# An attention and mixture-of-experts kernel: the first routing's steps re-timed between two merged loops

## The chip, the cores and the metric

The program runs on one core of one Trainium2 chip: TensorE (PE), VectorE (DVE), ScalarE (ACT), GpSimd (POOL), and SyncE (SP) which here only issues DMAs. The metric is the device time of one execution in microseconds, the median of the runs shown.

## The reference, cut to what matters

Attention runs in chunks of 64 positions over 8 batches and 8 heads; its output is the input of a router that sends each of 4608 tokens to one of 8 experts, each of them two matrix products with a ReLU between.

```python
scores = scale * np.matmul(q_c, k_c.transpose(0, 1, 2, 4, 3))
attn = np.exp(scores - max); attn = attn / (sum + 1e-09)
x = np.matmul(attn, v_c) ...                      # 4608 x 512
logits = x @ w_gate + modality_bias[modality_id]  # 8 experts
e_idx, gate_w = argmax, its softmax weight
for e in range(E):
    h = np.maximum(x[mask] @ w1[e], 0.0)
    out[mask] = gate_w[mask, None] * (h @ w2[e])
```

## The kernel before, in words

The tokens are 36 tiles of 128; a **round** r does the attention of tiles 2r and 2r+1, so there are 18 rounds. A round has `scores` (64 small products, called one round ahead), `differences` (row maxima and the subtraction on VectorE), `exps` (ScalarE, and then one addition `sr` on GpSimd that halves the row to be summed), `sums` (the row sums and their reciprocals `ris`, VectorE), `transposes`, `values`, `evict` (ScalarE), `rows` (one for each of the two tiles: products that transpose back and give the router's partial logits, and a VectorE multiplication `xr` by `ris`), `parts` (ScalarE copies `lp` of the partial logits) and `put` (the tokens to the DRAM table `xd`). The first eight rounds (`NPURE`) run alone, and are called the **lone rounds** here. The other ten are emitted piecewise by the generator `merge`, between the products of the experts, three steps a round (transposes; values and the next scores; rows).

The experts work in **slots** of 384 tokens. Slot s has eight **blocks** f; the weight slice of block f of slot s is g = 8s + f. A block runs `first` (12 products, in two halves with a `tick` between, then ReLU and its low part `hh`, `hl`), `second` of the block before (9 products), and `wsplit(g + 3)`, which splits a weight slice fetched by `fetch` into a high and a low part. A `tick` runs what `later` has put off and takes one step of `merge`. All weights arrive by SP's queue in the order of the code, three pair buffers deep.

Routing is done for groups of tiles: 8, 8, 12 and 8 (`GROUPS`). Each has a generator, `route0` or `route(g)`, kept in the list `jobs`; `scatter(g, ...)`, kept in `pooljobs`, issues one indirect DMA a tile into the token table `tab` from GpSimd. `advance()` takes one step of each job and each pool job; in the lone rounds `hook(r, k)` calls it at four places k of a round, in a slot the blocks do. `route0` has these steps: the logits (L354), the maxima and the one-hot `oh0` (L357 to L362), the ranks (`rank_tiles`, L365 and L341 to L343, and then twenty VectorE operations to `vm`, L389), a pause, and `got` (eight products, L395) with two small operations that give slot 0's token list. Both products are put into the bank `pairs[1]`, which `rows` of the odd tiles uses too. `gather 0` (GpSimd, L717) then brings slot 0's rows, and `split 0` transposes them. After group 1 (`route(1)`) the generator `early_table(1)` makes, in four steps, the list of slots 1 to 3. `scatter(0)` writes to the table in one no-dependency group, `scatter(1)` in another (L507), so that a scatter of one group waits for those of the other that were emitted before it.

`PREP` names what is called at the end of a block: `choose` runs the jobs to their end, `blank` and `locate` are SP's DMAs on the table, `settle` ends the scatters, `gather 1` and `gather 2` bring the rows of slots 1 and 2 into the one buffer `xg`. `split 1 0` and `split 1 2` transpose slot 1's rows (6 products each on a bank of `pair()`, and a ScalarE and a VectorE pass); `AMID` puts them into the middle of a `first`. `pair()` alternates two PSUM banks, `spare()` takes one for the ranks of a later route. The order of the instructions on each engine is the order of the code.

Of the kernel before, what the change touches and what calls it, by code (L numbers as in the profile page):

```python
# [35 lines left out]
NPURE = 8  # L36
# [4 lines left out]
    7: {1: ["fetch 2"], 2: ["lo 0", "hi 1"]},  # L41
}
AHEAD = 3
AMID = {6: "split 1 0", 7: "split 1 2"}

PREP = {
    0: {2: ["choose", "blank 1"], 3: ["settle", "locate 1"],
        4: ["gather 1", "head"], 5: ["locate 2", "locate 3"], 7: ["gather 2"]},
# [48 lines left out]
def attention_moe(ctx: ExitStack, tc: tile.TileContext, qkv, mod, cst, bias, wcat, wfst, void, out):  # L97
# [236 lines left out]
    def logits(a, b):  # L334
        sums_of_heads(0, a, b - a, lg0[:, a:b])
# [9 lines left out]
    def route0():  # L345
# [6 lines left out]
            return wk.tile([P, n, E], dt, name=name, bufs=1)  # L352

        logits(6, n)  # L354
        yield
        mx, fm = t2("gmx0"), t2("fm0")
        V.reduce_max(mx, lg0, axis=AX.X)  # L357
# [417 lines left out]
    def fetch(g, n=2):  # L775
        s, f = divmod(g, NF)
        if s not in ereg:
            expert(s)
        raw = rawr[g // 2 % 3][:, f % 2:f % 2 + n]
        SP.dma_start(raw, (wfst if s < NSPLIT else wcat)[ds(ereg[s], 1), :, f:f + n, :].rearrange("e p f c -> p (e f) c"))  # L780
        for i in range(n):
            raws[g + i] = raw[:, i]
# [62 lines left out]
    def second(ys, h, w, f):  # L845
        whi, wlo = w
        hh, hl = h
        for t, y in enumerate(ys):
            tsl = slice(t * P, (t + 1) * P)
            for i, (a, b) in enumerate(((hh, whi), (hh, wlo), (hl, whi))):  # L850
                PE.matmul(y, a[:, tsl], b[:, DM:2 * DM],  # L851
                          start=(f == 0 and i == 0), stop=(f == NF - 1 and i == 2))
# [18 lines left out]
    def slot(s):  # L871

        nt = tiles(s)
        end = max(s + 1, NSURE) * NF
        ys = acc[0:nt]
        pend = None
        if s >= NSURE:
            expert(s)
            locate(s)
            for f in (0, 2, 4):  # L880
                fetch(s * NF + f)
            gather(s)
            stash(s)
            place(s)
            for f in range(AHEAD):
                wsplit(s * NF + f)
            for k in range(NK):
                turn(s, k)
                part(s, k)
        for f in range(NF):  # L890
            g = s * NF + f
            if s == 0 and f in (2, 3):
                if f == 3:
                    fetch(g + 5)
            elif f % 2 == 0 and g + 6 < end:
                fetch(g + 6)
            h = first(xring[s % 2], W[g], g, nt * P)
            tick()
            advance()
            if s == 0 and f < 4:  # L900
                for k in ((2,), (3,), (4,), (5, 6))[f]:
                    wsplit(k)
            elif g + AHEAD < end:
                wsplit(g + AHEAD)
            advance()
            if s == 0:
                advance()
            if pend is not None:
                second(ys, pend, W[g - 1], f - 1)
                tick()  # L910
            pend = h
            for c in PREP.get(s, REGULAR).get(f, ()) if s < NSURE else ():
                call(c, s if s > max(PREP) else 0)
            advance(pe=spare())
        second(ys, pend, W[s * NF + NF - 1], NF - 1)
        tick()
        finish(s, ys)

# [2 lines left out]
    jobs, pooljobs, due = [], [], []  # L921
# [5 lines left out]
    def advance(lists=None, pe=None):  # L927
        for js in lists or (jobs, pooljobs):
            for j in list(js):
                if j in held:  # L930
                    if pe is None:
                        continue
                    rpbank[0], pe = pe, None
                    held.discard(j)
                got = next(j, "end")
                if got == "end":
                    js.remove(j)
                elif got == "rp":
                    held.add(j)
# [9 lines left out]
    def tick():  # L949
        for d in due:  # L950
            d[0] -= 1
        for d in [d for d in due if d[0] <= 0]:
            due.remove(d)
            d[1](*d[2])
        if merging[0] and next(steps, "end") == "end":
            merging[0] = False
# [13 lines left out]
    def hook(r, k):  # L970
        clock[0] = r
        advance()
        for c in PLAN.get(r, {}).get(k, ()):
            call(c)
# [8 lines left out]
    for r in range(NPURE):  # L983
        scores(r + 1, sb)
        hook(r, 0)
        differences(r + 1, sb)
        hook(r, 1)
        transposes(r, ts)
        if r:
            rows(2 * r - 2, pairs[0])  # L990
        exps(r + 1)
        values(r, ts)
        hook(r, 2)
        if r:
            rows(2 * r - 1, pairs[1])
        evict(r)
        if r:
            parts(r - 1)
            put(r - 1)
        hook(r, 3)  # L1000
        sums(r)
        if r == 0:
            setup()
    clock[0] = NPURE
# [1 line left out]
    wlo(1)  # L1006
    split(0, 0, sb)
    split(0, 2, pairs[0])
    rows(2 * NPURE - 2, pairs[1])
    sums(NPURE)  # L1010

# [107 lines left out]
```

## Time and profile before

| | us |
|---|---|
| median of 3 runs | 566.47 |
| lowest, highest | 565.35, 567.4 |
| the profiled execution | 567.62 |
| its span, first to last instruction | 565.8 |
| PE busy | 526.5 (93%) |
| VectorE busy | 357.6 (63%) |
| ScalarE busy | 241.8 (43%) |
| GpSimd busy | 166.6 (29%) |
| mean granted clock of TensorE | 0.986 |

The lone rounds take the span's first 73.5 us, slot 0 the time to about 160 us, and slots 0 and 1 carry the merged rounds; from about 184 us on there are experts only. In the rows below a round, a block or a step is found by its line: L240 scores, L246 and L247 differences, L255 `sr`, L259 and L260 sums, L268 transposes, L283 values, L300 and L302 rows, L310 parts, L833 first, L851 second, L758 split, L795 the low part of a weight. "Idle before" in a timeline is the time for which the engine did nothing ahead of the instruction, with what ended it; "issue" there means that no wait is seen.

### The profile page before, as it was taken

Reading aid. Unit: us, or ns where it says so; the run is one execution under the profiler, and the core shown is the slowest. Engines: PE = TensorE matmul, PEld = TensorE weight load, DVE = VectorE, ACT = ScalarE, POOL = GpSimd, SP = SyncE. Lnnn points to the kernel's source line nnn. Section 1 sums busy time; section 2 is a strip of 40 time slices with the busy share of each in tenths; the row PEclk is TensorE's granted clock in tenths of the full one; section 3 lists DMA queues with packets and bytes.
Section 4 is the critical chain, followed back from the end, with each engine's and each line's share of the span. In section 5 each row is a group of like instructions: output and inputs, shape, how many; then the busy total and the mean of one; then the engine's idle time right before and its main releaser. Section 6 shows DMA issues by size and latency. Waiting matters only on the chain.

```text
span 565.8 us, 12228 instructions
## 1 busy us (share of the span) xinstructions
PE 526.5 (93%) x4938; PEld 473.0 (84%) x4938; DVE 357.6 (63%) x590; ACT 241.8 (43%) x401; POOL 166.6 (29%) x186
## 2 busy tenths in 40 slices
PE   6786979779989999999999999999999999999993
PEld 3675878669878989899998998998899989989992
DVE  4567777766877787855656565564646556466750
ACT  3443544435545343534434444343344344344530
POOL 3332445723263675132220404123040301202101
PEclk9988899999999999999999999999999999999998
DMA  8996996399767429788766958677695856557500
GB/s 343 404 337 199 347 380 221 132 366 321 259 230 197 163 100 263 260 269 313 197 203 219 274 163 268 182 215 238 204 255 196 233 174 207 206 168 242 187 19 27
DMA packets 48626, 129.87 MB, mean 230 GB/s; under 512 B 7100, under 2 KB 23852, under 8 KB 39600
## 3 DMA queue, kind: packets, MB, share of 16 engines
q1 hardware_dynamic: 36592, 100.39, 54.2%
q0 software_dynamic: 7072, 19.18, 9.9%
q10 hardware_dynamic: 4896, 9.44, 4.4%
q8 instruction: 40, 0.66, 0.5%
q14 instruction: 26, 0.21, 0.1%
HBM read 101.95 MB, written 27.83 MB: 229 GB/s over the span
## 4 chain that ended last, share of the span: by engine, by line
PE 60%; issue 15%; DVE 4%; POOL 3%; ACT 1%; POOLq 0%; ACTq 0%; DVEq 0%
PE y L833 26%; PE sb L851 18%; PE t L851 9%; PE t L833 2%; PE y L300 2%; POOL out L866 1%; PE y L240 1%; DVE wl L795 1%; PE y L268 1%; POOL tab L504 1%; DVE mx L246 1%; PE y L283 1%; DVE xr L302 0%; ACT at L271 0%; DVE xl L761 0%
## 5 line engine op out<-in xcount | busy, mean ns | idle before, releaser
L795 DVE TENSOR_TENSOR wl<-raw,wh 128x1024 fp32r<-128x1024 f32 x104 | 127.3, 1225 | 34.0 <-ACT wh L791 34.0
L841 ACT ACTIVATE hh<-y 128x384 fp32r<-128x384 f32 (+1 forms) x92 | 43.4, 472 | 185.7 <-PE y L833 185.4
L833 PE MATMUL y<-xh,wh 128*128 128x384 f32 (+1 forms) x368 | 120.7, 328 | 0.0
L833 PE MATMUL y<-xh,wl 128*128 128x384 f32 (+1 forms) x368 | 120.7, 328 | 0.0
L833 PE MATMUL y<-xl,wh 128*128 128x384 f32 (+1 forms) x368 | 120.1, 326 | 0.0
L842 DVE SCALAR_TENSOR_TENSOR hl<-y,hh 128x384 fp32r<-128x384 f32 (+1 forms) x92 | 49.1, 534 | 103.2 <-ACT hh L841 103.2
L791 ACT CAST wh<-raw 128x1024 fp32r<-128x1024 f32 x104 | 108.2, 1042 | 0.3 <-issue 0.2
L866 POOL DMA_INDIRECT out<-yo,tk x37 | 38.1, 1031 | 228.2 <-DVE yo L865 200.1
L851 PE MATMUL sb<-wh,hh 128*128 128x512 f32 x208 | 82.7, 398 | 0.0
L851 PE MATMUL sb<-wh,hl 128*128 128x512 f32 x208 | 82.4, 396 | 0.0
L851 PE MATMUL sb<-wl,hh 128*128 128x512 f32 x208 | 82.0, 394 | 0.0
L833 PEld LDWEIGHTS y<-xl,wh 128*128 128x128 f32 x368 | 69.3, 188 | 3.6
L833 PEld LDWEIGHTS y<-xh,wh 128*128 128x128 f32 x368 | 69.4, 189 | 3.4
L833 PEld LDWEIGHTS y<-xh,wl 128*128 128x128 f32 x368 | 69.2, 188 | 0.0
L717 POOL DMA_INDIRECT xg<-xd,tk x37 | 41.9, 1131 | 17.4 <-issue 7.3
L851 PEld LDWEIGHTS sb<-wh,hl 128*128 128x128 f32 x208 | 39.0, 188 | 9.0
L504 POOL DMA_INDIRECT tab<-tg,pi x36 | 40.6, 1127 | 19.1 <-issue 11.0
L255 POOL TENSOR_TENSOR sr<-ex 128x512 f32<-128x512 f32 x18 | 23.4, 1302 | 73.3 <-ACT ex L253 73.2
L300 PE MATMUL y<-cs,xt 128*128 128x144 f32 x288 | 43.2, 300 | 1.3 <-DVE ex L247 1.3
L851 PEld LDWEIGHTS sb<-wh,hh 128*128 128x128 f32 x208 | 39.1, 188 | 5.7
L851 PEld LDWEIGHTS sb<-wl,hh 128*128 128x128 f32 x208 | 39.1, 188 | 4.8
L300 PEld LDWEIGHTS y<-cs,xt 128*128 128x128 f32 x288 | 40.1, 200 | 3.0 <-DVE ex L247 1.7
(226 smaller groups left out, 703.3 us busy)
## 6 DMA issues: line engine op xcount, KB each, us to landing
raw<-in_wcat SPq DMA_DIRECT2D x44, 1024.0 KB, 5.5
qk<-in_qkv SPq DMA_DIRECT2D x18, 1024.0 KB, 7.4
v<-in_qkv SPq DMA_DIRECT2D x18, 512.0 KB, 5.1
xd<-xr ACTq DMA_DIRECT2D x18, 512.0 KB, 5.5
raw<-in_wfst SPq DMA_DIRECT2D x8, 1024.0 KB, 8.5
xs<-xg SPq DMA_DIRECT2D x9, 768.0 KB, 7.6
xq<-xs SPq DMA_DIRECT2D x36, 192.0 KB, 4.4
xs<-xg SPq DMA_DIRECT2D x2, 512.0 KB, 6.5
```

Source lines behind the costliest of these rows:

```text
L240: PE.matmul(sp[c * 64:c * 64 + 64, u, h, :], b[us, 0, h, c], b[us, 1, h, c], start=True, stop=True)
L255: G.tensor_tensor(sring[r % 2][:, :, :, 0:32], exu[:, :, :, 0:32], exu[:, :, :, 32:64], ALU.add)
L300: PE.matmul(fp[:, p, 0:GWC], xt[:, p, :], gw[:, p, :], start=True, stop=True)
L504: w = G.indirect_dma_start(tab, bass.IndirectOffsetOnAxis(ap=pi[:, j:j + 1], axis=0), tg[:, j, :], None, bounds_check=E * CAP - 1, oob_is_ ...
L717: G.indirect_dma_start(xg[:, t, :], None, xd[0:n, :], bass.IndirectOffsetOnAxis(ap=tk[:, t:t + 1], axis=0), bounds_check=n - 1, oob_is_err ...
L791: A.copy(hi, raw)
L795: (G if pool else V).tensor_tensor(lo, raw, hi.bitcast(F32), ALU.subtract)
L833: PE.matmul(hp, a[:, ks], b[:, k, 0:n], start=(m == 0), stop=(m == 3 * NK - 1))
L841: A.activation(hh[:, 0:n], hp, AF.Relu)
L842: V.scalar_tensor_tensor(hl[:, 0:n], hp, 0.0, hh.bitcast(F32)[:, 0:n], ALU.max, ALU.subtract)
L851: PE.matmul(y, a[:, tsl], b[:, DM:2 * DM], start=(f == 0 and i == 0), stop=(f == NF - 1 and i == 2))
L866: w = G.indirect_dma_start(out, bass.IndirectOffsetOnAxis(ap=tk[:, t:t + 1], axis=0), yo, None, bounds_check=N - 1, oob_is_err=False)
```

## The change

`route0` pauses once more after its logits, so that in the lone rounds the maxima come after `differences` of round 5 instead of before, the ranks after `values` of round 5 instead of before `transposes`, and `got` after the scores of round 6 instead of before. `sums(r)` moves from the end of round r to behind the next round's `scores` and hook 0; the last, `sums(7)`, moves behind the two splits of slot 0. In slot 0 a block steps the routing jobs three times, not four, and the scatters five times, not four. `choose`, `blank 1`, `settle`, `locate 1` to `3`, `head` and `gather 1` come one block later, `fetch(8)` and `fetch(10)` too; `split 1 0` moves from block 6 to block 7, and `split 1 2` and `gather 2` from block 7 to behind slot 0's last `second`. `merge` itself, with its three steps a round, has no line in the diff.

```diff
--- before.py
+++ after.py
@@ -41,11 +41,11 @@
     7: {1: ["fetch 2"], 2: ["lo 0", "hi 1"]},
 }
 AHEAD = 3
-AMID = {6: "split 1 0", 7: "split 1 2"}
+AMID = {7: "split 1 0"}
+FIRSTS = {0: 6, 4: 8, 5: 10, 6: 12}
 
 PREP = {
-    0: {2: ["choose", "blank 1"], 3: ["settle", "locate 1"],
-        4: ["gather 1", "head"], 5: ["locate 2", "locate 3"], 7: ["gather 2"]},
+    0: {3: ["choose", "blank 1"], 4: ["settle", "locate 1"], 5: ["gather 1", "head"], 6: ["locate 2", "locate 3"]},
     1: {1: ["stash 2"], 2: ["place 2"], 3: ["gather 3"], 4: ["turn 2 0", "turn 2 1"],
         5: ["part 2 0", "part 2 1", "turn 2 2"], 6: ["part 2 2", "turn 2 3", "stash 3"], 7: ["part 2 3"]},
     2: {0: ["place 3"], 3: ["turn 3 0"], 4: ["part 3 0", "turn 3 1"], 5: ["part 3 1", "turn 3 2"],
@@ -352,6 +352,7 @@
             return wk.tile([P, n, E], dt, name=name, bufs=1)
 
         logits(6, n)
+        yield
         yield
         mx, fm = t2("gmx0"), t2("fm0")
         V.reduce_max(mx, lg0, axis=AX.X)
@@ -889,9 +890,9 @@
                 part(s, k)
         for f in range(NF):
             g = s * NF + f
-            if s == 0 and f in (2, 3):
-                if f == 3:
-                    fetch(g + 5)
+            if s == 0:
+                if f in FIRSTS:
+                    fetch(FIRSTS[f])
             elif f % 2 == 0 and g + 6 < end:
                 fetch(g + 6)
             h = first(xring[s % 2], W[g], g, nt * P)
@@ -904,7 +905,8 @@
                 wsplit(g + AHEAD)
             advance()
             if s == 0:
-                advance()
+                advance((pooljobs,))
+                advance((pooljobs,))
             if pend is not None:
                 second(ys, pend, W[g - 1], f - 1)
                 tick()
@@ -913,6 +915,9 @@
                 call(c, s if s > max(PREP) else 0)
             advance(pe=spare())
         second(ys, pend, W[s * NF + NF - 1], NF - 1)
+        if s == 0:
+            call("split 1 2")
+            call("gather 2")
         tick()
         finish(s, ys)
 
@@ -983,6 +988,8 @@
     for r in range(NPURE):
         scores(r + 1, sb)
         hook(r, 0)
+        if r:
+            sums(r - 1)
         differences(r + 1, sb)
         hook(r, 1)
         transposes(r, ts)
@@ -998,7 +1005,6 @@
             parts(r - 1)
             put(r - 1)
         hook(r, 3)
-        sums(r)
         if r == 0:
             setup()
     clock[0] = NPURE
@@ -1006,6 +1012,7 @@
     wlo(1)
     split(0, 0, sb)
     split(0, 2, pairs[0])
+    sums(NPURE - 1)
     rows(2 * NPURE - 2, pairs[1])
     sums(NPURE)
```

## Rows read from the trace of the kernel before

**Rows 1.** Windows: us, busy us of PE, PEld, DVE, ACT, POOL, clock, DMA.

```profile
73.50:184.00 110.50, 98.48 (x1698) 87.93 (x1697) 80.86 (x147) 54.09 (x99) 49.40 (x49) 1.00 0.74 259
...
184.00:556.00 372.00, 372.00 (x1931) 336.92 (x1931) 228.52 (x358) 153.67 (x241) 90.69 (x91) 1.00 0.65 206
```

**Rows 2.** PE's timeline, rounds 5 to 8: start, us, instruction, idle before, releaser.

```profile
48.54 0.24 PE L341 MATMUL y<-oh,ub 128*128 128x72 bf16 x1 [3.10 <-DVE oh L362]
...
57.02 0.34 PE L395 MATMUL y<-vm,xg 128*128 128x6 bf16 x8 [2.32 <-ACT lp L310]
...
58.39 1.63 PE L268 MATMUL t<-cs,ex 128*128 128x128 f32 x8
...
71.47 0.66 PE L758 MATMUL sb<-cs,xg 128*128 128x128 f32 x4 [0.91 <-DMA xg<-xd,tk]
```

**Rows 3.** Windows over round 6 and round 7 of the lone rounds.

```profile
57.29:64.26 6.97, 6.97 (x155) 6.41 (x152) 4.18 (x7) 3.29 (x6) 4.51 (x4) 0.76 0.89 315
...
64.26:70.18 5.92, 5.72 (x154) 5.27 (x154) 5.58 (x7) 4.15 (x8) 0.66 (x1) 1.00 1.03 400
```

**Rows 4.** VectorE's timeline in round 5.

```profile
45.07 0.69 DVE L259 TENSOR_REDUCE sm<-sr 128x16 f32<-128x528 f32 x1
...
45.79 0.25 DVE L260 RECIPROCAL ris<-sm 128x16 f32<-128x16 f32 x1
...
47.23 0.22 DVE L357 TENSOR_REDUCE gmx<-lg 128x8 f32<-128x64 f32 x1 [1.19 <-POOL lg L330]
...
48.40 1.22 DVE L246 TENSOR_REDUCE mx<-sb 128x16 f32<-128x1024 f32 x1
...
50.79 0.16 DVE L367 TENSOR_REDUCE top<-y 128x1 f32<-128x8 f32 x1
...
52.59 1.26 DVE L384 SCALAR_TENSOR_TENSOR col<-ge,col 128x8 f32<-128x8 f32 x1
...
55.32 0.20 DVE L389 TENSOR_TENSOR vm<-ge,val 128x48 bf16<-128x48 f32 x1
```

**Rows 5.** GpSimd's timeline in rounds 5 and 6.

```profile
52.56 1.27 POOL L255 TENSOR_TENSOR sr<-ex 128x512 f32<-128x512 f32 x1 [5.36 <-ACT ex L253]
...
58.72 1.24 POOL L717 DMA_INDIRECT xg<-xd,tk  x1 [4.89 <-DVE ris L260]
```

**Rows 6.** DMA issues from 50 to 80 us: median us to landing.

```profile
xg<-xd,tk POOLq DMA_INDIRECT x3, 9.4
```

**Rows 7.** PE's timeline, blocks 1 to 4 of slot 0.

```profile
82.70 1.18 PE L283 MATMUL y<-at,v 64*64 64x64 f32 x64 [1.10 <-ACT at L271]
...
104.02 1.09 PE L268 MATMUL y<-cs,ex 128*128 128x128 f32 x8 [2.65 <-ACT lp L310]
...
115.13 1.09 PE L268 MATMUL y<-cs,ex 128*128 128x128 f32 x8 [0.82 <-ACT lp L310]
...
121.71 0.34 PE L240 MATMUL y<-qk 64*64 64x64 f32 x5 [2.43 <-issue]
```

**Rows 8.** ScalarE's timeline, block 1 of slot 0.

```profile
81.91 0.26 ACT L457 ACTIVATE ge<-lg 128x64 f32<-128x64 f32 x1 [2.92 <-DVE lg L445]
```

**Rows 9.** GpSimd's timeline, blocks 0 to 2 of slot 0.

```profile
81.86 1.08 POOL L504 DMA_INDIRECT tab<-tg,pi  x1 [0.49 <-DVE gmx L444]
...
88.43 1.92 POOL L504 DMA_INDIRECT tab<-tg,pi  x1 [0.30 <-issue]
...
94.83 0.98 POOL L504 DMA_INDIRECT tab<-tg,pi  x1 [2.01 <-issue]
...
99.86 2.01 POOL L504 DMA_INDIRECT tab<-tg,pi  x1 [4.04 <-DMA tab<-tg,pi]
...
106.86 1.28 POOL L255 TENSOR_TENSOR sr<-ex 128x512 f32<-128x512 f32 x1
```

**Rows 10.** Windows over blocks 5 and 6 of slot 0.

```profile
126.04:135.43 9.39, 9.39 (x177) 8.63 (x175) 6.40 (x9) 5.00 (x9) 4.51 (x6) 1.00 0.91 309
...
135.43:145.93 10.50, 10.40 (x183) 9.51 (x182) 7.47 (x10) 5.67 (x10) 1.51 (x2) 1.00 0.96 344
```


## The prediction

> **What bounds the kernel now.** I read the windows by stage first. From 184 to 556 us TensorE is busy in all of the 372 us, so nothing in the change can shorten that stretch, which does the same products after the change; from 73.5 to 184 us it is busy for 98.5 of 110.5, so 12 us are idle [rows 1]. The question is therefore only how much earlier the saturated stretch begins, and every microsecond of TensorE's idle time that goes before it comes off the end. Then I read TensorE's timeline for its gaps. In the lone rounds the ranks stand in front of round 5's transposes and wait 3.10 us for the one-hot, `got` waits 2.32 us, and `split 0` waits 0.91 us for the gathered rows [rows 2]. Round 6, which follows two such gaps, is 6.97 us long at a granted clock of 0.76 (a mix of the two levels, 1.2 and 2.4 GHz); round 7 takes 5.92 at 1.00 [rows 3]. In slot 0 the values of block 1 wait 1.10 us for ScalarE's copies, the transposes of blocks 3 and 4 wait 2.65 and 0.82 for the copies `lp`, and 2.43 pass in block 4 with no wait seen ("issue") [rows 7]. VectorE, ScalarE and GpSimd are read for what releases these.
>
> **The lone rounds.** VectorE is the chain here. Before, it ends `sums(4)` at 46.04, then waits 1.19 us for GpSimd's logits, does the maxima from 47.23 to 48.40 (1.17), `differences(6)` from 48.40 to 50.79 (2.39), and the ranks' operations from 50.79 to 55.52, 4.73 us [rows 4]. After, `differences(6)` follows `sums(4)` at once, since its scores end near 45.4, ahead of which TensorE has no wait; the logits' latency lies beneath it. One operation of the rank chain on 128x8 takes 1.26 us where its neighbour takes 0.16; it runs from 52.59, beside GpSimd's `sr`, which takes 1.27 from 52.56 [rows 4, 5]. `sr(6)` moves some 2.4 us earlier with `differences(6)`, and the chain then comes after it, so I take 3.6 us for it (bounds 3.6 and 4.73). The sum: 46.04 + 2.39 + 1.17 + about 0.65 for the multiplication of tile 8 + 3.6 = 53.85 for the end of `vm`. From there to `got` there were 1.50 us (55.52 to 57.02), two multiplications and a copy; one multiplication has moved ahead, so 0.85 remain, and `got` takes 0.34: transposes(6) start at 55.05 instead of 58.39 [rows 2, 4]. That is **3.3 us** (2.2 if the slow operation only moves).
>
> TensorE does not come out of it without waits: the rank products wait for the one-hot after `values(5)`, the products of tile 9 wait behind the ranks, in the same bank, until VectorE has read them, and `got` now stands in front of transposes(6). Each I work out at about 1.2 us, beside VectorE's chain and so not added to it. Whether round 6 gets its 1.05 us back (6.97 less 5.92, [rows 3]) depends on the clock after these shorter gaps; I take half, **0.5** (bounds 0 and 1.05). `gather 0` follows `got`, so it is issued about 3.3 us earlier than 58.72 [rows 5]. If its landing takes the same 9.4 us [rows 6] it gains only those 3.3, and `split 0`, which would come 3.8 earlier and lose its wait of 0.91 besides, waits again; but fewer transfers are under way ahead of it. I take **0.4** beyond the 3.8 (bounds -0.5 and 0.9).
>
> `sums` moved: on VectorE `sums(r)` keeps its place between the same neighbours in most rounds, as `scores` is TensorE's work. It costs in one place: `sums(7)`, 0.94 us long by its like [rows 4], stands behind the low parts of slot 0's rows now, and the multiplications, copies and the ReLU of block 0 wait behind it. There VectorE has no slack, so **-0.9**. Lone rounds in sum: 3.3 + 0.5 + 0.4 - 0.9 = **3.3 us** (bounds 0.8 and 4.3).
>
> **Slot 0, blocks 0 to 4.** The routing's exponential `ge` (L457) sat on ScalarE in front of the copies of the transposes, and ScalarE waited 2.92 us there for VectorE's maxima [rows 8]; these copies end the 1.10 us of block 1 [rows 7]. With three steps a block `ge` is emitted behind these copies, and nobody else is behind it: **1.1**. `early_table`'s third step (eight small operations, near 1.4 us) stood ahead of the multiplications whose copies release block 3's transposes; now it stands behind them. Against that, `sr(9)` lies behind eight scatters, not six, and `sums(9)` holds VectorE longer. I take **1.0** of the 2.65 (bounds -1.0 and 1.6). The fourth step comes into block 3 instead, ahead of two weight splits and tile 20's multiplication: it costs 1.1 us of VectorE, most of which the earlier `sums(10)` pays, so **-0.3** (bounds -1.1 and 0.8).
>
> Why `sums(10)` comes earlier: GpSimd began the scatters at 81.86 and did the first six at a pitch of 1.31 us (88.43). Then one scatter of group 1 waited 2.01, the last of group 0 waited 4.04 behind it, and `sr(10)` was reached only at 106.86 [rows 9]. The two groups' scatters were emitted alternately, and each waits for the landing of the other's. With two pool steps more per block all eight of group 0 are out before the first of group 1, so that one such wait is left. Thirteen scatters at 1.31, one `sr` and one wait of about 3 make some 21 us from the first scatter to `sr(10)`, against 25.0 for twelve.
>
> The "issue" gap of 2.43 us in block 4 has no releaser that the change touches; it stays at its price, and counts nothing. Blocks 0 to 4 in sum: **1.8 us** (bounds -1.0 and 3.5).
>
> **The end of slot 0.** Block 6 with a split takes 10.50 us, block 5 without one 9.39 [rows 10]; block 6 loses its split, 1.1. Block 7 has one before and after. `split 1 2` behind the last `second` stands where the transposes had to wait for `lp` anyway; it takes the bank that values(15) wants next, and its low part must be read first: -0.3. So **0.8** (bounds 0 and 1.1).
>
> **Edits that cost nothing.** On SP's queue `blank 1`, `fetch(8)`, `locate` and `fetch(10)` move a block later; the loads of rounds 13 and 14 queued behind the blanks come earlier. `fetch(8)` is used after `first` of block 5, about a block and a half (14 us of 9.39 each, [rows 10]) after it is issued, and a landing under load took 9.4 [rows 6], so 4.7 us are spare; past these each microsecond delays the slices of slot 1. `gather 1` keeps its distance to `split 1 0`. `gather 2` comes some 3 us later, with the output's scatters behind it on GpSimd; its rows are turned four blocks on, over 37 us.
>
> **The sum.** 3.3 + 1.8 + 0.8 = 5.9 us earlier. Against the profiled execution of 567.62 that is 561.7; that execution lies 1.15 above the median of 566.47, so for the median I forecast **560.6**.
>
> **Rivals.** *The lone rounds give most of it back.* The three short gaps keep TensorE at half clock, the slow operation of the rank chain only moves, and the gather lands 9.4 us after it is issued. Then the first term is 2.2 + 0 - 0.5 - 0.9 = 0.8, the sum 3.4, the time 563.1. The 6.97 us of round 6 and the 9.4 speak for it; against it, two long gaps are gone. *The scatters do not get faster*: the waits belong to the queue and not to the groups. Then thirteen scatters take 13/12 of the 25.0 us, 27.1, and `sr(10)` ends about 5.5 us later than block 3's VectorE work, which my reckoning has ready some 21.5 us after the first scatter. That leaves 0.4 of 5.9: 566.1, no change. The first six at 1.31 speak against it. *The same place, slower*: GpSimd's scatters are held as the one at 99.86 (2.01 us instead of 0.98, [rows 9]), so 13 of 2.0, the `sr` of 1.3, and the wait of 4.04 in full make 31.3, 9.8 late: 3.9 slower than before, 570.4. It decides from 27.4 us between first scatter and `sr(10)` on. The Trainium skill (SBUF — State Buffer, the section on SBUF's two separate sides) says that VectorE and GpSimd share a port pair as an exclusive lock, and that a VectorE operation that holds it keeps GpSimd from writing a DMA's descriptors. By that rule more scatters among VectorE's weight splits are held, which would make this rival's time; this trace agrees in part: the 1.26 us operation beside `sr` was held, the scatter at 88.43 took 1.92 us, but five scatters before it kept the pitch of 1.31. *More comes*: the lone rounds give their upper bound and the waits on `lp` go, 8 us: 558.5.
>
> **How the numbers follow.** The forecast has 0.60, the lone rounds giving back 0.20, more 0.06, no change through the scatters 0.08, slower through them 0.06. About 0.3%, 1.7 us, is what a measurement of this kernel can tell from no change. Faster is then 0.60 + 0.20 + 0.06 = 0.86, same 0.08, slower 0.06. The forecast's own spread is near 2 us, 558.6 to 562.6. The range reaches over the first rival and part of the upper case, 557.2 to 564.6.
>
> **What would show it.** In the profile of after: no wait of TensorE for `oh` above 1.5 us; transposes(6) near 55; `split 0` reached near 66 to 67.5; first block's products near 69 to 70; the values of block 1 without a wait; eight scatters before `sr(9)` and one long wait on GpSimd; the transposes of block 3 with a wait under 2 us; the 2.43 still there; block 6 at 9.4. It is wrong if `split 0` waits over 2 us for its rows, if VectorE waits over 3 us for `sr(9)` or `sr(10)`, or if new gaps open after block 6.

## The result and the profile after

| | before | after |
|---|---|---|
| median of 4 runs | 566.92 | 561.33 |
| lowest, highest | 565.35, 567.4 | 559.09, 562.1 |
| the profiled execution | 567.62 | 561.35 |
| its span | 565.8 | 559.6 |

The ratio is 0.990, with an interval of 0.987 to 0.993: 5.6 us less by the medians, 6.27 by the profiled executions. The forecast was 5.9 by the profiled executions, 560.6 for the median. The total is right; several of its terms are not, and they cancel. What follows compares one execution of each kernel; how far other executions bear it out is said behind the table below.

The windows of after (us, then the busy time of PE, PEld, DVE, ACT and POOL, clock, DMA share, GB/s) have the same form as [rows 1].

```profile
70.00:184.00 114.00, 106.08 (x1739) 95.97 (x1739) 88.40 (x154) 56.52 (x104) 51.04 (x53) 0.99 0.75 262
184.00:550.00 366.00, 366.00 (x1895) 331.31 (x1894) 224.42 (x353) 151.81 (x237) 87.19 (x86) 1.00 0.65 206
```

From 184 us on TensorE is busy without a break, as before. So what was gained was gained ahead of it, and one can follow it by comparing the start of the same products in the two traces. They reach the scores ahead of the first edit that bites at 44.28 and 44.40 us, so the two can be compared. TensorE's timeline of after, in the lone rounds and in the first block, is the counterpart of [rows 2]:

```profile
49.71 0.19 PE L341 MATMUL y<-oh,ub 128*128 128x72 bf16 x1 [1.05 <-DVE oh L363]
...
51.37 1.25 PE L300 MATMUL y<-cs,xt 128*128 128x144 f32 x8 [1.28 <-DVE base L375]
...
54.77 0.34 PE L396 MATMUL y<-vm,xg 128*128 128x6 bf16 x8 [1.07 <-ACT lp L310]
54.98 1.07 PE L268 MATMUL t<-cs,ex 128*128 128x128 f32 x8
...
59.23 1.19 PE L240 MATMUL sb<-qk 64*64 64x64 f32 x64
...
66.13 0.33 PE L759 MATMUL sb<-cs,xg 128*128 128x128 f32 x1 [0.47 <-DMA xg<-xd,tk]
68.67 0.66 PE L759 MATMUL sb<-cs,xg 128*128 128x128 f32 x4 [2.21 <-DMA xg<-xd,tk]
...
70.71 0.43 PE L834 MATMUL t<-xh,wh 128*128 128x384 f32 x1
...
76.42 0.44 PE L834 MATMUL t<-xh,wh 128*128 128x384 f32 x1 [2.04 <-DVE hl L843]
```

Transposes(6) start at 54.98 instead of 58.39 (3.41 earlier), the scores behind them at 59.23 instead of 64.26 (5.03), `split 0` is reached 4.79 earlier, and there 2.68 us pass in waiting for the gathered rows instead of 0.91 and a part of the lead is lost: the first block begins 2.79 earlier (70.71 for 73.50), and block 1's products, which wait for `hl` behind `sums(7)`, 1.93 earlier.

Slot 0 of after, for [rows 7]:

```profile
77.83 1.91 PE L268 MATMUL y<-cs,ex 128*128 128x128 f32 x8
...
100.93 1.09 PE L268 MATMUL y<-cs,ex 128*128 128x128 f32 x8 [1.27 <-ACT lp L310]
...
113.11 1.09 PE L268 MATMUL y<-cs,ex 128*128 128x128 f32 x8 [2.51 <-ACT lp L310]
...
116.18 1.30 PE L240 MATMUL y<-qk 64*64 64x64 f32 x64
...
128.88 2.13 PE L300 MATMUL y<-cs,xt 128*128 128x144 f32 x16
...
138.30 2.12 PE L300 MATMUL y<-cs,xt 128*128 128x144 f32 x16
```

The 1.10 us ahead of block 1's values are gone, but the transposes before them (77.83) take 1.91 instead of 1.03. Block 3's transposes wait 1.27 instead of 2.65, block 4's 2.51 instead of 0.82. The break of 2.43 in block 4's scores is gone: 64 products in one piece at 116.18. Block 6 takes 138.30 less 128.88, 9.42 us.

GpSimd's timeline shows the scatters, for [rows 9]: the first, the last of the eight of group 0, the first of group 1, and the two `sr`.

```profile
80.05 1.09 POOL L505 DMA_INDIRECT tab<-tg,pi  x1 [0.49 <-DVE gmx L445]
...
89.62 0.98 POOL L505 DMA_INDIRECT tab<-tg,pi  x1 [0.31 <-issue]
90.63 1.29 POOL L255 TENSOR_TENSOR sr<-ex 128x512 f32<-128x512 f32 x1
93.15 1.00 POOL L505 DMA_INDIRECT tab<-tg,pi  x1 [1.23 <-DVE ris L260]
...
100.25 1.29 POOL L255 TENSOR_TENSOR sr<-ex 128x512 f32<-128x512 f32 x1
```

`sr(10)` comes 20.2 us after the first scatter, for 25.0 before. The wait of 4.04 for the other group's landing is gone, and no scatter waits longer than 1.23.

### The profile page after: what moved, and what is told of

Read it like the earlier page. It is cut to its first block, busy times and chain, and to the rows that moved or that the text cites. A ratio compares the mean times of both kernels' runs of the same rounds, so it can differ in the third digit from the quotient of the medians.

```text
span 559.6 us, 12222 instructions
## 1 busy us (share of the span) xinstructions
PE 527.3 (94%) x4937; PEld 473.7 (85%) x4938; DVE 358.4 (64%) x590; ACT 241.1 (43%) x401; POOL 164.8 (29%) x186
## 4 chain that ended last, share of the span: by engine, by line
PE 71%; issue 15%; DVE 7%; DMA 3%; POOL 2%; ACT 1%; POOLq 0%; ACTq 0%; DVEq 0%
PE y L834 26%; PE sb L852 19%; PE t L852 10%; PE y L300 4%; PE t L834 3%; DMA xg<-xd,tk 2%; PE y L268 2%; PE y L283 2%; PE y L240 2%; PE sb L240 2%; DVE mx L246 1%; POOL out L867 1%; PE t L283 1%; DVE xr L302 1%; DVE ex L247 1%
## 5 line engine op out<-in xcount | busy, mean ns | idle before, releaser
L796 DVE TENSOR_TENSOR wl<-raw,wh 128x1024 fp32r<-128x1024 f32 x104 | 128.7, 1239 | 33.9 <-ACT wh L792 33.7
L505 POOL DMA_INDIRECT tab<-tg,pi x36 | 39.2, 1090 | 13.6 <-issue 9.1
L300 PE MATMUL y<-cs,xt 128*128 128x144 f32 x288 | 41.3, 292 | 1.7 <-DVE base L375 1.3
L300 PEld LDWEIGHTS y<-cs,xt 128*128 128x128 f32 x288 | 38.2, 193 | 3.2 <-DVE base L375 1.4
```

The lines of the kernel that those rows point to most:

```text
L300: PE.matmul(fp[:, p, 0:GWC], xt[:, p, :], gw[:, p, :], start=True, stop=True)
L505: w = G.indirect_dma_start(tab, bass.IndirectOffsetOnAxis(ap=pi[:, j:j + 1], axis=0), tg[:, j, :], None, bounds_check=E * CAP - 1, oob_is_ ...
L796: (G if pool else V).tensor_tensor(lo, raw, hi.bitcast(F32), ALU.subtract)
```

## The experiments

The first four ran on one chip, the other eight on a second. On the first the kernel before takes 598.27 us (median of 28), so those totals are compared there alone. On the second before takes 566.92 (15 runs) in one series and 567.6 (22 runs) in the next, as in the comparison above.

**Lone rounds alone.** Kernel before, with the pause in `route0` and the moved `sums`; slot 0 untouched.

```diff
     logits(6, n)
+    yield
     yield
...
     hook(r, 0)
+    if r:
+        sums(r - 1)
...
-    sums(r)
...
     split(0, 2, pairs[0])
+    sums(NPURE - 1)
```

> The kernel before with the lone rounds' part of the change alone: the extra pause in the first routing and the moved sums; slot 0 as before. Theory A (the parts add): split 0 is reached near 65.4 us and waits about 2.7 us for the gathered rows, block 0's products begin near 70.7 (2.8 earlier than before), block 1's near 76.4 (1.9 earlier, since sums(7) costs 0.9), and from there on the trace is that of before shifted by 1.9: the 1.10, 2.65, 0.82 and 2.43 us waits of slot 0 stay, total 1.9 us less than before. Rival B (the gain of the lone rounds is eaten in slot 0, where GpSimd's scatters or VectorE set the time anyway): block 4's transposes come within 0.5 us of before's 115.1 and the total is within 0.5 us of before.

597.16 us, ratio 0.9991 (0.9955 to 1.0027): no difference on that chip. There `split 0` does not wait for its rows, in this trace or in the next three; here it is reached at 65.91.

**Slot 0 alone.** The change without those lines.

> The change without the lone rounds' part: slot 0's stepping, its later calls and fetches and the moved splits; the first routing's pauses and the sums as before. Theory A (the parts add): block 0's and block 1's products begin as before, 73.5 and 78.35; block 1's values wait under 0.3 us instead of 1.10; block 3's transposes wait about 1.3 instead of 2.65, block 4's about 2.5 instead of 0.82, the gap of 2.43 without a releaser in block 4 is gone, block 6 takes 9.4 instead of 10.5; total about 4.2 us less than before. Rival B (slot 0's part only takes back what the lone rounds' part brings forward): total within 1 us of before.

603.4 us, ratio 1.008 (1.0048 to 1.0112): slower on that chip. The view of TensorE's waits (engine, line, releaser: us in total, times, longest) shows what is new there:

```profile
PE y L283 <- issue: 11.6, 28, 1.1
PE y L240 <- issue: 5.8, 10, 1.1
...
PE y L268 <- ACT lp L310: 2.8, 2, 2.5
```

38 breaks without a releaser in the merged values and scores, 17.4 us together; the trace of before on the other chip has one, the 2.43 of [rows 7]. The kernels without slot 0's edits have them on this chip too, but fewer: 26 of together 12.7 us in the lone rounds alone, 23 of 9.7 with the eight products more (below). So the slot's edits may bring more of them, and that would make up the loss, but one trace of each does not show it. From 184 to 560 us of this run TensorE is busy for 368.33 of 376 us: the merged rounds reach to 206 us, and 4.44 are waited at 244.81; only from 246 on is it busy without a break. So the premise that nothing is idle from 184 us on fails on this chip, and a total there doesn't show what a part brings ahead of it. Why this chip makes such breaks is open.

**`sums(7)` back ahead of the split.** The change, with one line moved.

```diff
     wlo(1)
+    sums(NPURE - 1)
     split(0, 0, sb)
     split(0, 2, pairs[0])
-    sums(NPURE - 1)
```

> The change, with the sums of round 7 put back ahead of the splits of slot 0, where VectorE waits 2.77 us for the first split's ScalarE pass. Theory A: the 0.94 us of these sums then lie in that wait; block 1's products wait about 1.17 us instead of 2.04 for the low part of the ReLU, begin near 75.5 instead of 76.4, and the total is 0.9 us below the change's (ratio to before near 0.988). Rival B: VectorE's second weight split, which GpSimd's additions hold, and the first scatter keep their time, block 3's transposes come at the same time as in the change (100.9), and the total is that of the change.

600.18 us, ratio 0.9994 (0.9956 to 1.0032). The total decides nothing, and it shows besides that a near relative of the change gains nothing on this chip. The local effect is plain: block 1's products wait 1.17 us for `hl` instead of 2.04.

**Eight products more at the start.** Kernel before, with eight warm-up products of 64 columns, to see what the break in block 4 hangs on.

```diff
+    for _ in range(8):
+        PE.matmul(pairs[1][:, 1, 0:64], warm[:, 0:P], warm[:, 0:64], start=True, stop=True)
```

> The kernel before with eight more warm-up products of 64 columns at the start, while TensorE waits for its first data: 16 instructions more ahead of everything on TensorE's queue. Theory A (the gaps without a releaser stand at fixed counts of TensorE's instructions, 256 apart, because the next instructions are not there yet): the gap of round 4 comes after 54 of the 64 score products instead of 62, the one of block 4 after 51 instead of 59, each 2 to 3 us long. Rival B (a DMA or another engine stops TensorE there): the gaps stay at the same products, 62 and 59, or go.

595.98 us in a single run. Breaks without a releaser stand in the lone rounds too. In TensorE's timeline of before (on the other chip), scores in the first rounds and in round 4:

```profile
15.71 1.04 PE L240 MATMUL sb<-qk 64*64 64x64 f32 x55 [2.05 <-issue]
...
38.19 0.30 PE L240 MATMUL sb<-qk 64*64 64x64 f32 x2 [2.73 <-issue]
```

and of this kernel, in the first rounds and in round 4:

```profile
17.39 1.98 PE L242 MATMUL sb<-qk 64*64 64x64 f32 x63 [2.71 <-issue]
...
40.01 0.44 PE L242 MATMUL sb<-qk 64*64 64x64 f32 x10 [2.35 <-issue]
```

The break stood ahead of the last 2 of 64 products and stands ahead of the last 10 now; the other stood ahead of the last 55 and now of the last 63. Both moved by just the eight products that were added. So these breaks hang on the count of TensorE's instructions and not on the work at the place. From 15.71, the end of one break of before, to 21.68, the end of the next, the trace has 128 products and 127 weight loads, 255 instructions together. The page of the profile lists a queue of its own for instructions on the same DMA engines ("q8 instruction", 40 packets of together 0.66 MB before, 41 and 0.67 here). The Trainium skill (Runtime: NRT & Kernel Launch, Instruction fetch mechanics) says that an engine fetches its instructions by a DMA queue in blocks of 256, at a cost that is "mostly hidden". The fixed counts agree with that; the price does not, as 2.35 and 2.71 us here show. Block 4's break wasn't seen in this run, although the fetches are in their old place.

**The change again**, as the base of the second series.

> The change itself, as a measure for the runs beside it on the same chip. On a chip like that of the first comparison: ratio to before 0.990, split 0 waits 2.7 us for its rows, block 1's products 2.04 for the low part of the ReLU, block 4's transposes 2.5, no gap without a releaser in block 4.

559.43 us, ratio 0.9898 (0.9863 to 0.9934): the gain repeats. Here too block 4's transposes wait long (2.64) and the break is gone.

**One weight split a block later.** Block 3 of the change does two; here block 4 takes one of them.

```diff
-            if s == 0 and f < 4:
-                for k in ((2,), (3,), (4,), (5, 6))[f]:
+            if s == 0 and f < 5:
+                for k in ((2,), (3,), (4,), (5,), (6, 7))[f]:
```

> The change, with the sixth weight slice split in block 4 instead of block 3, so that VectorE reaches tile 20's multiplication a weight split (1.2 us, and the 1.1 us for which GpSimd's addition holds it) earlier. Theory A (the gap in block 4 is TensorE's wait for its next instructions, and the wait of block 4's transposes ahead of it covers it): the transposes wait 0.3 to 1 us instead of 2.5 and the gap of about 2 us after 59 of the 64 score products is back; the sum of the two stays between 2.5 and 3.3 and the total within 0.6 us of the change's. Rival B (the change removed the gap by another way, by the later fetches or the scatters): no gap, block 5 begins 1.5 to 2.2 us earlier and the total is 1.5 to 2.2 below the change's.

558.61 us, ratio 0.9859 (0.9815 to 0.9903). TensorE's timeline:

```profile
98.31 1.09 PE L268 MATMUL y<-cs,ex 128*128 128x128 f32 x8 [1.23 <-ACT lp L310]
...
108.56 1.09 PE L268 MATMUL y<-cs,ex 128*128 128x128 f32 x8 [0.72 <-ACT lp L310]
```

The wait of block 4's transposes falls to 0.72, and the break doesn't come back. So it was not merely covered by that wait: the theory that the two are one time is out, and the change had taken the break away in another manner.

**`fetch 2` later.** One of the weight loads that are under way beside the first gather goes from hook 1 to hook 3 of round 7.

```diff
-    7: {1: ["fetch 2"], 2: ["lo 0", "hi 1"]},
+    7: {2: ["lo 0", "hi 1"], 3: ["fetch 2"]},
```

> The change, with the weights of slices 2 and 3 fetched two hooks later in round 7 (after the last products of the round instead of after the differences), some 4 us later and so behind the gather of slot 0's rows. Theory A (the rows land late because this megabyte and the others share the DMA engines with them): split 0 waits 1 to 2 us less for its rows (0.7 to 1.7 instead of 2.7), block 0's products begin 1 to 2 us earlier, the second slice's split in block 0 does not wait, total 1 to 2 below the change's. Rival B (the gather's landing is set by its own descriptors or by the earlier transfers): the wait stays within 0.4 of 2.7 and the total is the change's.

562.8 us, ratio 0.9888 (0.9848 to 0.9928). `split 0` still waits 0.41 and 2.20 us. From 54 to 70 us the gather lands after 8.4 us (median), in after 8.1, and the DMA engines carry 374 and 377 GB/s: one load the less changes nothing, since others follow.

**Both.** `sums(7)` ahead and `fetch 2` later.

> The change with both edits at once: the sums of round 7 ahead of slot 0's splits and the fetch of slices 2 and 3 two hooks later. Theory A: 0.9 for the sums and 1 to 2 for the gather, 1.9 to 2.9 below the change. Rival B: later waits of slot 0 (block 4's gap, GpSimd's scatters) take it back, under 0.8 below the change.

558.16 us, ratio 0.9849 (0.9782 to 0.9917). Block 1's products wait 1.17 us instead of 2.04, as on the other chip; the gathered rows are waited for 1.93 us. The intervals of these three runs and of the change overlap, so their totals don't tell them apart; what they show is in the traces.

**Only the fetches later.** Kernel before, with `fetch(8)` and `fetch(10)` one block later and nothing else.

```diff
-            if s == 0 and f in (2, 3):
-                if f == 3:
-                    fetch(g + 5)
+            if s == 0:
+                if f in (0, 4, 5, 6):
+                    fetch({0: 6, 4: 8, 5: 10, 6: 12}[f])
```

> The kernel before with one part of the change alone: fetch(8) and fetch(10) one block later in slot 0. Theory C (the gap of 2.43 us in block 4 is TensorE's wait for its next 256 instructions, which are slow to come because fetch(8), sent with the loads of v and qk some 7 us ahead of it, fills the DMA engines): block 4's transposes still wait about 0.8 us, the gap after 59 of the 64 score products is under 0.6 us, the total about 2 us less than before. Theory A (a long wait of the transposes is what covers the gap): the transposes wait 0.8 and the gap stays near 2.4, total within 0.6 us of before.

567.22 us, ratio 0.9986 (0.9955 to 1.0017): no gain, although block 4's break is gone (its 64 scores run in one piece at 122.26). GpSimd's timeline shows where it went:

```profile
102.72 0.98 POOL L504 DMA_INDIRECT tab<-tg,pi  x1 [5.45 <-DMA tab<-tg,pi]
106.49 0.98 POOL L504 DMA_INDIRECT tab<-tg,pi  x1 [2.79 <-DMA tab<-tg,pi]
...
110.07 1.31 POOL L255 TENSOR_TENSOR sr<-ex 128x512 f32<-128x512 f32 x1
```

The two waits of a scatter for the other group's landing are 5.45 and 2.79 (4.04 and 1.40 before), so `sr(10)` comes 29.4 us after the first scatter (80.72 to 110.07) for 25.0. VectorE waits 7.11 us for it (2.81 before) and TensorE 2.75 for `differences` (0.54). Neither theory foresaw that: the break hangs on when the fetches come, as one had it, but here the time went into the scatters of the two groups, which wait for each other; in the change, where they don't, it was kept. Why the landings took longer is open; the loads of later rounds had moved up on SP's queue.

**The queues empty around the gather.** The change, with `fetch 2` at hook 3 and the loads of `qk` that `differences` of rounds 7 and 8 issues put behind `fetch(4)`.

```diff
-        load_qk(r + NB)
+        if r not in (7, 8):
+            load_qk(r + NB)
...
+    load_qk(7 + NB)
+    load_qk(8 + NB)
```

> The change, with SP's queue nearly empty while slot 0's rows are gathered: the loads of qk for rounds 10 and 11 and the fetch of slices 2 and 3 come behind round 7's last products. Theory A (each small packet of the gather waits its turn behind large ones of the other queues, so that the landing takes 8 to 9 us as long as any large transfer is under way, and moving one fetch alone changed nothing): the third gather lands about 4 us after its issue, split 0 waits under 0.5 us for its rows instead of 2.7, block 0's products begin about 2.2 us earlier, total 1.5 to 2.5 below the change's 0.990 of before (0.986 to 0.987). Rival B (the gather takes its 8 to 9 us by itself): the wait stays over 2 us, the total that of the change or above, if the later loads are missed.

558.4 us, ratio 0.9822 (0.9765 to 0.988). TensorE's timeline:

```profile
65.56 0.65 PE L760 MATMUL sb<-cs,xg 128*128 128x128 f32 x4 [0.51 <-DMA xg<-xd,tk]
...
73.55 0.44 PE L835 MATMUL t<-xh,wh 128*128 128x384 f32 x1 [2.05 <-DVE hl L844]
...
109.13 1.09 PE L269 MATMUL y<-cs,ex 128*128 128x128 f32 x8 [2.62 <-ACT lp L311]
```

The wait for the rows falls from 2.68 to 0.51. It is 1.78 to 2.69 us in after and in the five traces of this chip that have the change's lone rounds and these loads of `qk` in place, and none in the next kernel. Block 1's products start at 73.55 for 76.42, but that shows little by itself: the kernel with one weight split later, whose lone rounds are the change's, has them at 74.02. The DMA issues from 54 to 70 us (KB each, median us to landing) of after:

```profile
xg<-xd,tk POOLq DMA_INDIRECT x3, 8.1
```

and of this kernel, with 306 GB/s carried in place of 377:

```profile
xg<-xd,tk POOLq DMA_INDIRECT x3, 6.8
```

So on this chip the large loads beside the gather make it land late, and it takes several of them out of the way to see it. Its median of 6.8 is not the 4 us that the theory expected of the third gather. And what the engines carry is not all of it: on the first chip they carry 385 GB/s from 54 to 70 us of the lone rounds alone, and the rows are there in time. The total's interval meets that of the change (0.9863 to 0.9934).

**All three.** That kernel, with `sums(7)` ahead of the split and the weight split a block later.

> The change with the emptied queue, the sums of round 7 ahead of slot 0's splits, and the sixth weight slice split in block 4. If the three add: 2.2 from the gather, 0.9 from the sums, 1.8 from the split, 4.9 below the change, ratio to before near 0.981. If a later wait takes part back (weights that land late in block 0, GpSimd's scatters): 2 to 3 below the change, 0.985.

555.66 us, ratio 0.978 (0.9737 to 0.9824): 2.2% under before, and under the change, as the intervals lie apart. Block 1's products start at 73.26 with a wait of 1.17 for `hl`; block 4's transposes wait 0.73; in slot 0 0.97 and 0.21 remain as breaks without a releaser.

**The lone rounds alone, on the second chip.**

> The lone rounds' part alone once more, on this chip. Theory A (the parts add): split 0 waits about 2.7 us for its rows, block 1's products begin about 1.9 us earlier than before, slot 0's waits of 1.10, 2.65, 0.82 and the gap of 2.43 stay, total 1.9 below before (0.9966). Rival B: slot 0 takes it back, total within 0.6 us of before.

564.2 us, ratio 0.9923 (0.9884 to 0.9962). By the ratio that is 4.4 us of 567.6 (2.2 to 6.6), by the medians 3.4; the forecast had 3.3. The 1.9 that the pair of traces gives them (0.9966) lies just outside that interval. What the slot brings beside it is the rest of the change's gain, 1.4 us by the two ratios (0.9923 less 0.9898) and 4.1 by the medians (7.49 less 3.4), which doesn't settle its size. Its trace, though of an execution 3 us above the median, shows which waits belong to slot 0's edits, since they are back:

```profile
102.31 1.09 PE L268 MATMUL y<-cs,ex 128*128 128x128 f32 x8 [2.63 <-ACT lp L310]
...
113.92 1.09 PE L268 MATMUL y<-cs,ex 128*128 128x128 f32 x8 [0.81 <-ACT lp L310]
...
119.91 0.33 PE L240 MATMUL y<-qk 64*64 64x64 f32 x5 [1.82 <-issue]
```

## Why the prediction was right, and where its terms were wrong

The total came out by luck: a break that was to stay brought 2.5 us, and that covered what the gather and slot 0 fell short of. The earlier start of the same products in the two traces, from stage to stage, against the terms:

| term | forecast | measured | from |
|---|---|---|---|
| transposes(6) | 3.3 | 3.41 | 58.39 to 54.98 |
| clock of round 6 | 0.5 | 1.62 | transposes(6) to the next scores, 5.87 to 4.25 |
| `split 0` | 0.4 | -2.2 | lead of 5.03 at the scores, 2.79 at block 0 |
| `sums(7)` | -0.9 | -0.86 | lead of 1.93 at block 1 |
| **lone rounds** | **3.3** | **1.9** | |
| block 1 to block 4's transposes | 1.8 | 0.1 | lead of 2.02 at 113.11 |
| break in block 4 | 0 | 2.5 | lead of 4.57 at the rows behind it |
| end of slot 0 | 0.8 | 1.6 | lead of 6.2 at the end |
| **sum** | **5.9** | **6.2** | |

One execution stands on each side of this table. In the other traces the first row holds: from the scores at 44.28 to transposes(6) 14.10 to 14.11 us pass in the four traces with the lone rounds of before, and 10.58 to 10.98 in the ten with the new ones. The clock's row does not: the stretch that takes 5.87 before takes 4.27 in the kernel with only the fetches later, which has the same lone rounds, and 4.25 to 4.85 in after and on the second chip with the new ones. And the lone rounds alone gained 2.2 to 6.6 us by their runs, not 1.9. So how the total divides between the lone rounds and slot 0 is not settled; which waits went and which came is.

**The rank chain was read rightly.** The 1.26 us operation on 128x8 takes 0.17 now that no `sr` runs beside it, and the chain from 50.20 to the end of `vm` takes 3.68 us (3.6 taken). In VectorE's timeline of after:

```profile
52.04 0.17 DVE L385 SCALAR_TENSOR_TENSOR col<-ge,col 128x8 f32<-128x8 f32 x1
```

The three waits that were to stay on TensorE are there, 1.05, 1.28 and 1.07 us, for about 1.2 each. The clock term was mis-sized: I took half of the difference between two whole rounds, while the part behind `got` alone lost 1.62 in this pair. Round 7 was no measure of a round without loss either: its values are broken in two (18 and 46 products, 0.20 idle between).

**The gather was the step that failed in the lone rounds.** It was issued 2.24 us earlier (56.48 for 58.72), not 3.3: it follows `got`, and `got` itself came only 2.25 earlier (54.77 for 57.02). The 3.3 were those of transposes(6), which gained about one us more because the scores no longer lie between `got` and them; I had put the one's lead down to the other. And the rows landed 8.1 us after their issue (median), with the DMA engines at 377 GB/s. The last rows were there 9.34 us after the third gather's issue (59.33 to 68.67), for 9.90 before: 0.56 gained where 0.9 was taken. So block 0 could begin 2.24 and 0.56 earlier, 2.8 in place of the 4.2 forecast, and whatever TensorE had gained beyond that, the clock's part too, went into the wait for the rows. I had bounded this term at -0.5; -2.2 lies outside. The prediction said that it would be wrong if `split 0` waited over 2 us, and it waits 2.68; that part of it is wrong, and the kernel with the queues empty shows the cause. It is one of the three conditions of the rival in which the lone rounds give most of it back; the other two did not come.

**Slot 0's edits did what they were to do, and two costs took it.** Block 1's values lost their wait. But the transposes ahead of them took 0.88 more: TensorE had just waited 2.04 us, and the window from 77.8 us on shows it at a granted clock of 0.50, the lower level of 1.2 GHz (before, from 79 to 81 us, it was 1.00). Such a wait doesn't always bring that: of the six traces in which it is 1.67 to 2.05 us, these transposes take 1.91 in four and 1.03 in two. In the end the values of block 1 lead by 1.50 us, less than the 1.93 ahead of them, so the 1.1 forecast came to nothing.

```profile
77.80:79.80 2.00, 2.00 (x10) 1.97 (x9) 1.89 (x8) 0.00 (x0) 1.60 (x3) 0.50 0.84 335
```

Block 3's transposes gained 1.38 of wait (1.0 taken), by the mechanism named: the multiplications whose copies release them stand ahead of `early_table`'s third step now, whose small operations ran from 101.60 on before and run from 101.15 on after. In VectorE's timelines of before and of after:

```profile
103.04 1.28 DVE L302 TENSOR_TENSOR xr<-y,ris 128x512 f32<-128x512 f32 x2
...
99.96 1.28 DVE L302 TENSOR_TENSOR xr<-y,ris 128x512 f32<-128x512 f32 x2
```

`sr(10)` came 20.2 us after the first scatter for about 21 forecast, and `sums(10)` no longer waits for it (2.81 before). That paid for the fourth step: the two weight splits of block 3 begin 3.10 us earlier, as block 3's transposes did (3.09). But block 4's transposes lost 1.07 of that, for 0.3 taken, at the edge of the bounds. The splits in VectorE's timeline of before, then VectorE's timeline of after with `sr(11)` from GpSimd's, tell why:

```profile
111.88 2.35 DVE L795 TENSOR_TENSOR wl<-raw,wh 128x1024 fp32r<-128x1024 f32 x2
...
108.69 0.17 DVE L563 TENSOR_TENSOR taken<-taken,usum 128x8 f32<-128x8 f32 x1
108.78 3.43 DVE L796 TENSOR_TENSOR wl<-raw,wh 128x1024 fp32r<-128x1024 f32 x2
...
109.05 2.07 POOL L255 TENSOR_TENSOR sr<-ex 128x512 f32<-128x512 f32 x1 [3.77 <-ACT ex L253]
...
112.13 1.27 DVE L302 TENSOR_TENSOR xr<-y,ris 128x512 f32<-128x512 f32 x2
```

The last small operation of `early_table` stands ahead of the two splits, as expected. But the splits take 3.43 us where they took 2.35: `sr(11)`, now free of the scatters, runs beside them from 109.05 and itself takes 2.07 (1.38 before). The 1.08 are what block 4's transposes lost. That collision was not in the sum.

**The break in block 4** was counted as fixed because nothing that the change touches releases it. That was the wrong test: a break with no releaser can still depend on a resource. The windows ahead of the scores of before and of after, one from each trace, differ in what the DMA engines carry: 395 GB/s from 114 to 118 us before,

```profile
114.00:118.00 4.00, 3.18 (x68) 2.62 (x70) 2.50 (x6) 1.91 (x5) 1.35 (x1) 1.00 1.03 395
```

and 136 from 112 to 116 after, since `fetch(8)` is issued at 113.83, behind the blanks, where it stood at 110.29 with two loads behind it.

```profile
112.00:116.00 4.00, 2.90 (x66) 2.64 (x70) 2.44 (x6) 1.93 (x5) 0.00 (x0) 1.00 0.48 136
```

With the fetches alone moved, the break goes; with them left in place, 1.82 of it stays, and 2.92 in the lone rounds alone on the first chip. That it hangs on when the fetches come is shown by these.

What TensorE waits for stands in the DMA queues. Over windows of 0.2 us they have one packet of 16 KB of the instruction queue each (packets, MB, share of the 16 engines): before from 119.4 us on, in the break; the lone rounds alone again from 117.4, in theirs; after from 114.4, ahead of its scores at 116.18.

```profile
q8 instruction: 1, 0.02, 29.2%
...
q8 instruction: 1, 0.02, 29.6%
...
q8 instruction: 1, 0.02, 43.4%
```

The share makes 0.93 us of one engine for the first, which the trace has from 119.41 on; TensorE goes on at 121.71, 1.37 us after its end. It is the same elsewhere: in before, after and the eight traces of the second chip, each of the 43 breaks without a releaser behind the warm-up ends 1.20 to 1.62 us after the end of such a packet. And the scores of block 4 stop where theirs comes late: in the three traces with a break of 1.82 to 2.92 it starts 0.5 to 1.8 us behind the first of them, in the other eleven 1.0 to 3.3 us ahead, and at most 0.23 stays. One of these eleven, the eight products more, has the fetches in their old place. So the break is a wait for a load of instructions. Why that load starts late is not shown; that it stands behind other transfers fits the 395 GB/s against 136.

**The end of slot 0** had less from block 6 than the 1.1 forecast. The 10.50 of [rows 10] run past the first of block 7's products in TensorE's timeline of before:

```profile
145.67 0.43 PE L833 MATMUL t<-xh,wh 128*128 128x384 f32 x1
```

So block 6 was 10.24 us long (135.43 to 145.67), the split's price 0.85 beside block 5, and 0.83 of it came off (9.41 after, from one block's first products to the next's). `split 1 2` cost nothing for the 0.3 subtracted: behind slot 0's last `second` it fills the 0.82 us for which the transposes waited there, and from that `second` to them 2.84 us pass for 3.17. The rest, some 0.5, came in small waits before and behind. **The rivals on the scatters** fell: eight in a row kept their pitch of 1.3 but for one of 1.7, and only two of thirteen took over 1.2 us.

## What to carry to other kernels

Bringing a chain forward brings its DMA forward into other traffic, so a gather's landing should be priced from what else is under way at its new time, and large loads that can wait should go behind it, if the chip shows the wait. A stall with no releaser is not a constant: if it sits at a fixed instruction count, look in the DMA queues for the packet of instructions just before its end, and at what they carry ahead of that. Freeing GpSimd from one wait lets its vector work collide with VectorE elsewhere, so the next overlap belongs in the sum. And the stages of one pair of traces can be off by as much as the terms they are to check: a second trace of the same stage is cheap.

## What the hardware did that I had not expected

- TensorE stops for 0.2 to 2.9 us at fixed counts of its instructions; eight products more moved two such stops by exactly eight products, and 43 of them end 1.20 to 1.62 us after a 16 KB packet of the instruction queue.
- Some small operations on VectorE stretch many times over beside an addition on GpSimd: a 128x8 operation takes 1.26 us before and 0.17 after, and after, a cast of 128x8 takes 2.00 us beside `sr(9)` where it took 0.17. Others do not: the three from 50.20 to 50.86 of after take 0.16 to 0.23 beside `sr(6)`. The Trainium skill (SBUF — State Buffer, the section on SBUF's two separate sides) has the two engines share a port pair as an exclusive lock; the rows that stretch agree.
- The same kernel takes 566.92 us on one chip and 598.27 on another, with breaks of 0.2 to 1.1 us in runs of small products on the slower. On the slower, neither part of the change made the kernel faster.
